# The first two token groups' activation on ScalarE and GpSimd, in place of one VectorE operation, with a new order of issue

## The chip, the cores and the metric

One core of one Trainium2 chip runs the kernel. The metric is the device time of one execution in microseconds (us); lower is better. Five engines work in parallel, each through its own queue in program order: PE (TensorE, matmuls; its weight loads are listed as PEld), DVE (VectorE), ACT (ScalarE), POOL (GpSimd) and SP (SyncE, which here issues the DMAs). They meet through semaphores.

## What is computed

A gated linear attention with complex decays, followed by a two-layer block with a leaky activation. Shortened:

```python
# q, k, v, a_re, a_im: (B, H, S, D) = (4, 8, 768, 48)
mag = np.sqrt(a_re * a_re + a_im * a_im)
scale = np.minimum(mag, 0.999) / (mag + 1e-06)
a_re_n, a_im_n = a_re * scale, a_im * scale
for t in range(S):
    new_re = ar * S_re - ai * S_im          # ar, ai: row t of a_re_n, a_im_n
    new_im = ar * S_im + ai * S_re
    S_re, S_im = new_re + outer(k[t], v[t]), new_im
    y[t] = q[t] @ S_re
x = y.transpose(0, 2, 1, 3).reshape(3072, 384)   # tokens x (heads * D)
h = x @ w_in                                      # w_in: (384, 2048)
g = np.maximum(h, 0.0) + alpha * np.minimum(h, 0.0)
return g @ w_out                                  # w_out: (2048, 384)
```

## The kernel before

**Tasks.** The program is a set of Python generators. Each `yield` marks a step: the engine, a size for a planner and what the step waits for. The code after it issues the step's instructions. The planner itself is not in the file, only its result: ORDER, a string of some 4,500 letters, one letter for each step. `Plan.run` walks the string and advances the task of that letter, so the string fixes the order in which every engine's queue gets its instructions. The yielded sizes and the `Ring` objects (buffer counts) do nothing at run time. Waits on the chip come from the tiles that the instructions read and write.

The letters: A to I are the nine gate tasks (decays and phases of a batch's tokens); J loads q, k, phases and decays of each unit; K and L load rows of v; M brings in the pieces of the weights and alpha; N and O turn the weights' 64-bit words into float32; P to m are the 24 attention units of 128 tokens each; n loads x; o is the two-layer block (`all_mlp`); p and q belong to the last three groups, which are computed by another scheme with fewer multiplications.

**Units.** A unit multiplies q and k by phases and decays on VectorE (tiles KQ, WQ; L742, L744, L797), forms masked products of q and k level by level on TensorE (ps_lv, L759), masks them (A; L773, L782), transposes k (ps_kt, L868), updates the state (ps_kv, L880; St, L916 on ScalarE and L918 on VectorE) and gathers the unit's output in ps_y (L900, L930). The output is copied (L944) and sent to DRAM (ysc), from where a group's x is loaded (xT).

**The two-layer block.** Tokens are handled in groups: `sizes = [1, 1, 2, 2, ...]` units of 128 tokens, so groups 0 and 1 have 128 tokens and the others 256. For a group m and each of 16 slices f of the 2048 features, `features` issues three matmuls into ps_h (L978, two buffers), a ScalarE relu of -h into the group's place in g_sb (L985), and one VectorE operation (L987) that multiplies this by the column `al_1` (1 - alpha) and adds h from PSUM: relu(-h) * (1 - alpha) + h is the activation. Then `outputs` issues the matmul of the slice before (L997, into ps_o) that adds its part to the result. In `all_mlp` the output matmul of f-1 stands behind the ps_h matmuls of f. From group 1 on, the first output matmuls belong to the group before.

**GpSimd's work.** Before the change it has a step of the weights' conversion (L596), small products of the gate tasks (L396, L416, L418, L477, L480, L488, L490, L492; of these, the larger forms run on VectorE), memsets, and sums in the last three groups (L1160).

Of the kernel before, what the change touches and what calls it, by code (L numbers as in the profile page):

```python
# [27 lines left out]


ORDER = (  # L30
    "AAJMMAABAJAAAAAAAAAAAAAAAAAAAAMMMBJMAAAAAAAAAAKANAOAAAABAAANAAAKANNNABAMAJNBKOAKBOOKAABMAKABAAALOAAB"
# [3 lines left out]
    "OCNOOLCNOPCNKOMNNCPQPDJCQDLCDNQPPDQQQLCDQDKQQMCLNDQDOKPQQMODQLOOJQJDKQJDOLCQnOJOLDDJQNJOQLQLOOoLoDDC"
    "QLoQRQoLQQLQooooQQCoQDKNJooooRoMQoQCRCCoooooQoRDQQQCODDCONNCooRQRLoDCLRoMoLoCRRLCoooooCJoRDKCRKooooo"
    "RCDoRQLCDLCoooCoRKoOLCDJCQDCCoLDCRRDDCooooooLCQCooCLCoCoCoLCLCCCLCRCCLCKOCRCRLoCooCRRRCRRoRRCoCRCQQC"
    "CRCQCCoRKCRQRQQCQOORRoRCCQCCooRRCNQDoLoDLoNoDNoooNDoEDNNoEOJoDJRJDRLoooooDDoLDRRRLDRRLRDNDNEJDJSDDRo"
    "oJDESDEDSRDRJESSnJSoLESDoLoLODJSSJDSDLLTSDJoELoooooSSSDLoLooooJSSoDDDoSEDLoooSToSoJooJSSSDoSSDSSoooo"
    "ooSTSDETooooTToSEEoEDoooooSDToSEDTSESSSSDooLDTLoooLEEDSLToLSLoooooDLELoTJDSSSDoooooTTSDSESSSLoDooooo"  # L40
    "SEEDTLLoTKoooooDDDToTEJLDDDDoooooTEUJTDKoDoooKTToDoLoToooTLoUoDJoTLToooToEJoDonooToDEoDTKoUoDJooToUo"
    "EoEUTUEoETEDDDJTooUooDoUUoDooToToTTDoLoLoULoLDULLoooUUoDoLooooDoULoLoELooooLoUULoTLUTLJoooooFUEUoETT"
    "TUUUUTTTUooooTToUETUUFEoUEooooEoUVoUEoooooVVKJJUUEUUEUUoFooLEFLoUoLEUFJVUELoVJoUJooooVJEoFVEJEVoEUoo"
    "oUUUEVoEUoLoVVLEoooEoLEoVEJooooJVEWoFEnVVLoVELoLoooEoKVVEoELVEoJFooooJWoVoVFooWLooLVVEEWoLWVoLWVEFJV"
    "VVJEooVoVoooEKoWKoJEoooVEWWooVWoVoEFWVVVEVVEWELWEELooFEELoWLEoEoLoWWLVLoWEEEEVLLooooooLWEWLEoLEFELEK"
    "FFVVVooWooLooVVVVVFFFVLXKEoEWooooooEWWEEWWJoWWJoooWoEJWoWJoFJWoEWFFWWWWoEoELoLEoJoLoEoFXEooooFooooXo"
    "ooooKXWXLXFWoXoGGXLoXooooJWoLXoLWoFWXoXWFXWoFWXFWWoWXoXFFoFLoXoGFJFnGooooXXoJFoFLoLXXXXLGFLoooooXLFX"
    "XXoGoLFGFLoooooooFXoooGFoJoYJXoJFoJXFGKoooXFYFXoXFYJFooooGXXXYoYXLYFooLXFYFKoLoYoYLXXFZLFXLoXYXFLoXX"
    "XoooYXoFGLGFYYLoYGoFJoYFYJoooFoFZoLFoJoYJGKooooFJGYFYLooYYYLoJYYZGLLFoooooZLoFGYZYZoYZYKJFZZooooYFoZ"
    "YoYFGZYYFYFFYYFZFLFZFFLoYLoooZLooLoFFFFFYFZLFZYYYLFoZLYYFLYoooFZYLaZFLoFoooZZZZoYZZLZoGYFFLLoooZoZGo"  # L50
    "LGoFZJoZFFFGJoooooFooZFFZZFZZZGLoonoFLooLaoFoLoooaJoLoZoaJGoLZooaJaGoaoHoLZZLaaZoHGGoGZGZGGaZLGaLooo"
    "ooaZGaLoaJoZaZaooooGJoHaooHGoooaoaGLaHoooLoGLaaJaHoaJaaJoooooHoGbaoaGHoooaoGaobbJKHoaGaoaoaGaaHoLKoG"
    "JoboLGobLGoLGoooGbLoHGHbLboJbHoGJLaoLbbGLooooGoGHobLGaLaHbLGbabLaabaaGoLaooooLGbboGoGHbGooooJbGbGGKo"
    "bbboJobJbGGbcbbJobGGoooboGcbooooGbGoHbGbGcbbbLGcGLoooGbLcGHcGGJoboJcoLJGGGobLGccLGoobKcbLobHLbobbLoc"
    "obHoGHGdbLGHooooccocGoJoJHoooLcocdJooLconJHLoooocLcHoccccoccLGoJdcGGooocodHocHoHdHoHcGGGcoooGooocGGc"
    "GccccodGLLoooGcodooooLoddJoooLocdoLoIHIoHLdooooLHooLHdcoLdcoLdcLocJHcocddoHoHooKcoooILdocoLHoIHdcdLH"
    "LddoIKdooooJdoIddJoddKdHoHooodoHdoIoHedHHodeHIdddodoHLeHLoLoIHodLHoHLHeIHoLdLoooeeJHeHLoLdddHoooeeoH"
    "JHdedHLoJooooeIoLIeLeoeJddoLHoooLeeoLoHdIHeodJoHIHoooeeoJeeeeoeJeoeIJeoenJHIHoooeJIoeooHeHoHfeeoeHfe"
    "eoLLHoHHJHoHHeHoLfeoLILJHHHHofLooooofeLHfeHfLeHKoeIeLoKffLeHoooooefHeoeLgIIfogJLooooIoooffofoHJILooo"
    "ooHLffoJIoJfHHoooooKHofofJooLfffffofKoJgooHofgIoooggoIHIofofHIoIIoofoHKfooHofogfffoffggoLHLoLogoLoHI"  # L60
    "oLgoooILofnoIfgLgLgLfffoLggJoLgfKoooofooooIgLogfooLfIfofggggggogoohgogIhhLJJJIIhIooooogogoIIoogggggg"
    "oLILogoJIoJgIohJgIILgIgooohLIIgoJgIoIghILhIoIghILoLhhIooooIoIhIoJoLihILJooohhohLoLohLohoooLioJIIoLho"
    "LoJiJooohohooJhhiohhihJhihnoIIIhIoIIhIIIIooohIoIhIioIhihhhhhIihoLihLLLohhhLIIIIIiooooLohhiILiIoLiILo"
    "hLoooiiIoLohihohoLIoooILiIiLoLiiiiiioJioJioIIiIoooioiojoioIiiijIiiJooLojLoJoIoJoLjoooiLoIioLojIjiiiI"
    "jiiooooojjooooLojLiiJoooojLopoLjojiiLoooJjoLoojjJLojLLoooooJojLojooJjjjjjJojjJopjojookkkoojojooojjkj"
    "jojjokLkoLkLokJokoLokLoLoookLjooLjkJkokLLokkLoooLokooooLojjjLokjkjojkjjkojkkLlkookkopkJokJpoookokook"
    "oklkkkkLkLoookJlooLoLolooJokJopoJoLllJklnkLllokoooooklolokooollkkLLLolkoololoooJoLloJoLoooLlmlololoo"
    "oloLoLlooolLmooomololloolpmooolomlomopoomoomomoooomooomoollllllmmomoolomomoooolmoonoolllmmomlmomlmol"
    "lomomoooooooomLooLooooLoLoooLoooooooLoqLoooLooLomLooooLooLooLomLoooooooopooooomoooomoooooooooooooooo"
    "oooooooomomomoomoomomoooomomomoqlmqlmqmmmqqmqoooooqqoqoooooqoqqoqooqoqqooqoqqoqoqooqooqqoooooqoqqoqo"  # L70
    "ooooooooooqoooqoooqqoqqoqooooooooooqqooqoooooqqoqqoqooqoqooqoqqoqqqqqqqqoooooooooooqoqqoqoqooqooqooq"
    "oqoqooqoqoqoooqqqoqqonoooooooooooooooqooqqoqoqqoqqooooooooooooqqoqoqoooqooooooooooooqqqooqooqoooqoqq"
    "oqooooooooqqoooooooooqoooooooooooqooqoooqqoooqoqqqoqooooooooqoqoooqoqooooqqoqqoqooqoqooqqqoqoqqqqqqq"
    "ooooqoooooooqoqqoqooqqqoqoqooooooooooooqqqqqqoqqoooooooooooooooooqqqqoqqoqqooooooooooooooooooqoqqqoq"
# [30 lines left out]
def kernel(  # L105
# [863 lines left out]

    def features(m, f):  # L970

        n = sizes[m] * P
        for kk in range(NK):
            e = yield PE(n * 1.68e-3, ("x", m), ("w_in", f), takes=() if kk else (R["h"],))
            if kk == 0:
                p = ps.tile([P, MT], F32, tag="h", name="ps_h", bufs=2)[:, 0:n]
# [1 line left out]
            nc.tensor.matmul(p, lhsT=w_in_sb[:, f // 2, kk, f % 2 * P:(f % 2 + 1) * P], rhs=x_of[m][:, kk],  # L978
                             start=(kk == 0), stop=(kk == NK - 1))
# [5 lines left out]
        nc.scalar.activation(gt, p, AF.Relu, scale=-1.0)  # L985
# [1 line left out]
        nc.vector.scalar_tensor_tensor(out=gt, in0=gt, scalar=al_1[:, f:f + 1], in1=p,  # L987
                                       op0=ALU.mult, op1=ALU.add)
# [272 lines left out]
```

## Time and profile before

| | |
|---|---|
| time, median of 3 runs | 823.86 us (821.32 to 829.38) |
| profiled execution: time | 820.38 us |
| profiled execution: span from first to last instruction | 818.6 us |
| TensorE matmul busy | 681.1 us (83%), 11680 instructions |
| TensorE weight load busy | 539.0 us (66%) |
| VectorE busy | 693.9 us (85%), 1191 instructions |
| ScalarE busy | 520.3 us (64%), 1307 instructions |
| GpSimd busy | 222.2 us (27%), 293 instructions |
| mean granted TensorE clock | 0.968 |
| shares of the chain of waits that ended last | PE 65%, DVE 14%, DMA 10%, ACT 4% |

How to read what follows: a row of the profile names the line of the kernel, the engine, the operation, the tile written and the tiles read with their shapes, the count, then busy us and mean ns of one, then the engine's idle time just before such operations and what ended it. A duration can overlap the next one of the same engine, since operations are pipelined; the distance between two starts is what one occupies. The forty digits of a slice view are tenths of busy time in forty equal parts of the span. A chain of waits is followed back from the last instruction: each piece is what the next one had to wait for.

### The profile page before, as it was taken

What the parts mean: (1) busy time and instruction counts of PE and PEld (TensorE: products, weight loads), DVE (VectorE), ACT (ScalarE), POOL (GpSimd) and SP (SyncE); (2) the same over time, 40 slices, a digit from 0 to 9 for tenths busy, and PEclk for the clock granted to TensorE, in tenths of its full rate; (3) what the DMA queues carried; (4) which work ended last, traced back from release to release, by engine and by line L of the source; (5) the groups of instructions that cost most, each with busy time, mean ns of one, the idle gap of its engine ahead of it and who ended that gap; (6) DMA issues with size and microseconds to landing.
All of it is one profiled execution on the core that took longest, in us unless ns stands there. A gap on an engine that the chain in (4) does not pass through costs nothing.

```text
span 818.6 us, 27870 instructions
## 1 busy us (share of the span) xinstructions
PE 681.1 (83%) x11680; PEld 539.0 (66%) x11680; DVE 693.9 (85%) x1191; ACT 520.3 (64%) x1307; POOL 222.2 (27%) x293
## 2 busy tenths in 40 slices
PE   0003128659998999999999999999999999999997
PEld 0003126537776777767777777777777777899997
DVE  5999999999989899999999989998787775456574
ACT  8777998669666777876876697555756544312121
POOL 7231343051604310531245054003200000233342
PEclk9999659979999999999999999999999999999999
DMA  8594895593689589738865867787566622101000
GB/s 242 176 294 128 266 296 158 177 253 101 182 235 197 140 194 272 174 90 279 195 168 141 253 160 180 223 197 184 117 182 134 153 77 56 44 1 40 1 21 20
DMA packets 186598, 130.99 MB, mean 160 GB/s; under 512 B 74728, under 2 KB 176872, under 8 KB 186088
## 3 DMA queue, kind: packets, MB, share of 16 engines
q1 hardware_dynamic: 186472, 129.20, 59.3%
q8 instruction: 92, 1.51, 0.8%
q14 instruction: 34, 0.28, 0.1%
HBM read 100.82 MB, written 35.71 MB: 167 GB/s over the span
## 4 chain that ended last, share of the span: by engine, by line
PE 65%; DVE 14%; DMA 10%; ACT 4%; SPq 2%; issue 2%; POOL 1%; DVEq 0%; ACTq 0%; POOLq 0%
PE ps_o L997 19%; PE ps_h L978 18%; PE ps_m L1172 7%; PE ps_lv L759 5%; PE ps_y L1097 4%; PE ps_h L1097 4%; PE ps_y L900 3%; DVE KQ L797 2%; PE ps_kv L880 2%; PE ps_y L930 2%; DMA VL<-in_v_dram 2%; DVE gate L507 2%; PE ps_kt L868 1%; DVE gate L416 1%; DMA T<-decs 1%
## 5 line engine op out<-in xcount | busy, mean ns | idle before, releaser
L978 PE MATMUL ps_h<-xT,w_in_sb 128*128 128x256 f32 (+1 forms) x960 | 227.0, 369 | 2.1 <-DVE w_in_sb L600 1.6
L997 PE MATMUL ps_o<-w_out_sb,g_sb 128*128 128x384 f32 x576 | 222.1, 501 | 4.8 <-DVE g_sb L987 4.7
L978 PEld LDWEIGHTS ps_h<-xT,w_in_sb 128*128 128x128 f32 x960 | 170.9, 195 | 51.3 <-DVE w_in_sb L600 2.2
L797 DVE TENSOR_TENSOR KQ<-KQ,T 96x1024 f32<-96x1024 f32 x120 | 148.4, 1237 | 25.8 <-PE ps_lv L759 19.2
L997 PEld LDWEIGHTS ps_o<-w_out_sb,g_sb 128*128 128x128 f32 x576 | 102.5, 191 | 44.9 <-DVE g_sb L987 6.5
L985 ACT ACTIVATE g_sb<-ps_h 128x256 f32<-128x256 f32 (+1 forms) x160 | 57.9, 362 | 73.0 <-PE ps_h L978 72.2
L759 PE MATMUL ps_lv<-WQ 96*32 96x32 f32 x2304 | 34.4, 203 | 83.6 <-DVE WQ L742 70.2
L759 PEld LDWEIGHTS ps_lv<-WQ 96*32 96x32 f32 x2304 | 26.3, 116 | 105.9 <-DVE WQ L742 71.0
L916 ACT ACTIVATE St<-St,T 96x48 f32<-96x48 f32 x352 | 84.0, 325 | 4.6 <-DVE St L918 4.3
L987 DVE SCALAR_TENSOR_TENSOR g_sb<-g_sb,al,ps_h 128x256 f32<-128x256 f32 (+1 forms) x160 | 71.3, 446 | 13.7 <-ACT g_sb L985 13.1
L1160 POOL TENSOR_TENSOR sums<-g_sb 128x128 f32<-128x128 f32 x48 | 21.8, 475 | 185.5 <-DMA VL<-in_v_dram 110.6
L416 POOL TENSOR_TENSOR gate<-gate 128x72 f32<-128x72 f32 x42 | 34.5, 822 | 133.7 <-ACT gate L446 130.9
L596 POOL TENSOR_SCALAR top<-top 128x768 f32<-128x768 f32 x16 | 44.1, 2755 | 74.6 <-ACT top L588 63.2
L820 ACT COPY WQ<-KQ 96x1024 f32<-96x1024 f32 x48 | 50.0, 1041 | 18.9 <-DVE KQ L797 18.3
L416 DVE TENSOR_TENSOR gate<-gate 128x576 f32<-128x576 f32 (+5 forms) x84 | 50.7, 604 | 1.1
L900 PE MATMUL ps_y<-A,VL 64*48 64x64 f32 x2304 | 41.9, 220 | 4.4 <-issue 4.3
L900 PEld LDWEIGHTS ps_y<-A,VL 64*48 64x48 f32 x2304 | 39.0, 122 | 6.8 <-issue 6.7
L507 DVE TENSOR_TENSOR gate<-gate 128x1152 f32<-128x1152 f32 (+2 forms) x36 | 42.8, 1220 | 0.8 <-POOL gate L492 0.7
L1135 ACT ACTIVATE rl<-g_sb 128x256 f32<-128x256 f32 x24 | 10.0, 416 | 50.0 <-DVE g_sb L1128 50.0
L773 ACT ACTIVATE A<-ps_lv,columns 128x64 f32<-128x64 f32 x144 | 37.4, 336 | 6.2 <-PE ps_lv L759 5.9
L836 ACT COPY W<-KQ 96x512 f32<-96x512 f32 x48 | 30.8, 641 | 16.2 <-DVE KQ L797 8.7
L759 PE MATMUL ps_lv<-KQ,W 96*32 96x32 f32 x1536 | 24.7, 204 | 18.5 <-ACT W L836 17.4
(168 smaller groups left out, 1355.7 us busy)
## 6 DMA issues: line engine op xcount, KB each, us to landing
T<-decs SPq DMA_DIRECT2D x48, 384.0 KB
PP<-phs SPq DMA_DIRECT2D x24, 387.0 KB
KQ<-in_q_dram SPq DMA_DIRECT2D x48, 192.0 KB
decs<-gate SPq DMA_DIRECT2D x7, 1152.0 KB
phs<-gate SPq DMA_DIRECT2D x14, 576.0 KB
KQ<-in_k_dram SPq DMA_DIRECT2D x40, 192.0 KB
vsc<-in_v_dram SPq DMA_DIRECT2D x48, 144.0 KB
VL<-vsc SPq DMA_DIRECT2D x48, 144.0 KB
```

What stands on the lines that cost most here:

```text
L416: on(4 * k).tensor_tensor(out=m, in0=w[:, 1::-1].unsqueeze(2).to_broadcast([P, 2, 2, k]), in1=pairs_of(u), op=ALU.mult)
L507: TT(out=m[:, a], in0=U5[:, 1 + a], in1=turned(off3, o)[:, a].unsqueeze(1).unsqueeze(3).to_broadcast([P, L // 2, nb, 2]), op=ALU.mult)
L759: nc.tensor.matmul(t[64 * i + j:64 * i + j + HC // 2, p], lhsT=keys(n, g), rhs=queries(n, g), start=True, stop=True)
L797: nc.vector.tensor_tensor(out=x, in0=x if x0 is None else x0, in1=m, op=ALU.mult)
L900: nc.tensor.matmul(o, lhsT=Vp[h][64 * i:64 * i + 64, s, e_ * D:(e_ + 1) * D], rhs=a, start=False, stop=False)
L916: nc.scalar.activation(St[:, n], before[:, n], AF.Copy, scale=T[0:D2, n, TL - 4 + s:TL - 3 + s])
L978: nc.tensor.matmul(p, lhsT=w_in_sb[:, f // 2, kk, f % 2 * P:(f % 2 + 1) * P], rhs=x_of[m][:, kk], start=(kk == 0), stop=(kk == NK - 1))
L985: nc.scalar.activation(gt, p, AF.Relu, scale=-1.0)
L987: nc.vector.scalar_tensor_tensor(out=gt, in0=gt, scalar=al_1[:, f:f + 1], in1=p, op0=ALU.mult, op1=ALU.add)
L997: nc.tensor.matmul(sums[0], lhsT=gt[:, c * P:(c + 1) * P], rhs=w_out_sb[:, f], start=(f == 0), stop=(f == NF - 1))
L1097: nc.tensor.matmul(o, lhsT=lhs, rhs=rhs, start=(at in (0, 5)), stop=(at in (4, 8)))
L1172: nc.tensor.matmul(banks[k][:, half], lhsT=lhs, rhs=rhs, start=(j == 0 and half == 0), stop=(j == NF // 2 - 1 and at in (2, 3, 5, 6)))
```

## The change

For groups 0 and 1 (`m < ASIDE`) VectorE's operation is left out. Beside the relu, ScalarE copies h from PSUM into one of two halves of a new SBUF tile, `beside`, after which the ps_h buffer is free. GpSimd multiplies the relu's result by the column, in place, and then adds the copy. That is one ScalarE and two GpSimd instructions more and one VectorE instruction less for each of 2 x 16 slices. The small tile that a first, otherwise unused ScalarE activation wrote is now a part of `beside`. The string ORDER is another one throughout: 4607 letters in place of 4543, the 64 added ones being steps of task o.

```diff
+ASIDE = 2
...
 ORDER = (
-    "AAJMMAABAJAAAAAAAAAAAAAAAAAAAAMMMBJMAAAAAAAAAAKANAOAAAABAAANAAAKANNNABAMAJNBKOAKBOOKAABMAKABAAALOAAB"
...
+    "AABBMJAAAAAAAAAMAAAJAAAAAAABAAAAAAAAAMMMAAAAAABABAAKAANJAABKAKOAAAANMAAKBAAJNNAAKOAAKNOOMANBAABKABAN"
...
-        lv=2, misc=1, y=1, h=2, o=1).items()}
+        lv=2, misc=1, y=1, h=2, o=1, hc=2).items()}
...
-    nc.scalar.activation(consts.tile([P, 1], F32, tag="first", name="first"), bias_two, AF.Abs_reciprocal_sqrt)
+    beside = consts.tile([P, 2, P], F32, tag="beside")
+    nc.scalar.activation(beside[:, 0, 0:1], bias_two, AF.Abs_reciprocal_sqrt)
...
         nc.scalar.activation(gt, p, AF.Relu, scale=-1.0)
+        if m < ASIDE:
+            ra, r = r, (yield ACT(n, takes=(R["hc"],)))
+            hc = beside[:, f % 2, 0:n]
+            nc.scalar.copy(hc, p)
+            R["h"].put(r)
+            yield POOL(1.4 * n, ra)
+            nc.gpsimd.tensor_scalar(out=gt, in0=gt, scalar1=al_1[:, f:f + 1], scalar2=None, op0=ALU.mult)
+            r = yield POOL(1.4 * n, r)
+            nc.gpsimd.tensor_tensor(out=gt, in0=gt, in1=hc, op=ALU.add)
+            R["hc"].put(r)
+            return gt, r
         r = yield DVE(n + 45, r, first=True)
         nc.vector.scalar_tensor_tensor(out=gt, in0=gt, scalar=al_1[:, f:f + 1], in1=p,
                                        op0=ALU.mult, op1=ALU.add)
```

More of the change, by code (lines that the diff above doesn't have):

```diff
@@ L35 @@
[L35 to L74, printed above, removed]
@@ L75 @@
-    "oqoooooooooooooooooqqooooooooooooqoooqoqoooqoqqoqqoooooooooooqqqooooooqoqqoqqooqoqooqoqqqqqooooooooo"
-    "ooqoqqoqooqoqooqqoqqqqqqqqqqqqqqqqqqqqqqqqq")
+    "AABBMJAAAAAAAAAMAAAJAAAAAAABAAAAAAAAAMMMAAAAAABABAAKAANJAABKAKOAAAANMAAKBAAJNNAAKOAAKNOOMANBAABKABAN"
+    "KANOKAOMLALABBNNLBAAOLAAAKABBLOAAKBBLAABAAMAABLAAAKBALAABBBLAAAAABAOOABAAMBANAAAAAKALBAAABABABBBNBNB"
+    "OCNCBJBNNOLJBOKBONBOOBNBNOCBOBCPCPPJKKMKKBCLBBMBCPKBPKCLBBBPPBBBPOLBBJBPCLJOBPBPCOOKBPBBJBPPBCCPBPCB"
+    "PPBBBNPCBCPPNNBPMMKBBBCPPJPBBBBPBPCPPBPBPBCPPBCBBBBBPCBPPBPPCCLCBBBLLBPBNLPCLNLONCNPPPDONNJDCOCLCNOJ"
@@ new lines @@
+    "COOJMCCNCNJCNOCJOCQDKCLCDMQDCJPDNNQDMNQQCDQNJDQPOQQDOQPPPOOPCJDQQLNQKDCKODQJNnLNNMDDCOLQLQRJOLQoOLLD"
+    "DQKQOOoMQKoQQQKoRQooQCQKooQooQoCQDKQooCoooQCDoooCRDDooCROooQoooRoRDCCCODRoooooooQoQoCRRoooCooCRoQoLC"
+    "RRDJooRQCLooCDLCoCoLCoRoCJooCLQooooooLCRQLCCCLCCCDLooCRCoooooCLCDCOLCDRLoCoCOJoLoooooRRooCCCCDLCDoRR"
+    "RCooooooRCRRQQRRQCCDCCooCQoCCRLCQRoRCQooooOORQQCCJCRCRRRRooCRoQNRDNDNDNDNNDRRLDEoEDLDRJOJDoRJDRoJoDO"
+    "oooRLDoooooDnNELLoDSJDENJRooDESDooooooDSRDRJESSJoLSLSoJSSJDLooooSDJJTSSDLESKoSDLEKSooSoJoooooESJDooT"
@@ new lines @@
+    "DJDLDDDoooSoSSSSSSEooooDKSSSDKoTooLEELTKSLEoooooTTTLoTooEDEoooooSoSTEEDEoooooooSooSDTSoSSSDLTooSLoDo"
+    "oLTDoToDoSLTooLoooLDDoSSLoSoDLooSDSEoSoSSoSooLDEoLDDDoooooTDoLooUJTooooLoToJEJUTJTELTLDDDooTJoooooTT"
+    "TDLoTnoooooooooDDoEEEUoooEDTToooDoUoTDDooooUUoUToDTEDoEooooooTooEEoTDDDToUTJoDoooooooooTToLoDDDLoUoo"
+    "LDoUDoooooLoooooUTULoUTooLULooLUoULEoUFoooooULToUTEJUUTLTLUooToEFToTTUoEUTELoULUEoooooUoEUVooooUoEUE"
+    "FJVVoFJEJoooooUoEUJUEUJoUUEoLFUKoEoJVEoLoEVLEJoooUUVLEFVEUVKUoULVoELoUUVVEUooooELoEVEoKooooVEWoJFEVV"
@@ new lines @@
+    "LoEJooEoWEnoLoVLoELooooLoVVLFVJJEoEoooooVoWVFLELoooVVWoJVoJWoEWEVEVooVEVWVoVoooEWWoVFoVEWoooooVEEVEV"
+    "EVEEVFFFWEEWVLWoLWLEEEoKWWELoooooVELoWLoELVEooooKEoELoWFFJVWLVWEVLoEFKoooLWVoEVoWEEEWoWLVVVEWLoWWLWo"
+    "oooVoFLoEoFJJoooWoWoFoWEFFWWoWEWWLLEJFJooooooXJoEoooJXoFooooXKoLWXLoooooWXJFXGXLLWWWoLXXoGXWWooooooX"
+    "FXoFXWooFWWXFWoLoXXFoFFoLXoJGooonoFoJYXGLXoFLoJXXGoooooXFXoXLGoLXXFGLooooXFoXLFooGoooFXYoJXoJFoJoYGF"
+    "oooooooFoJXoFoXFXXFXXYXoLGXLYYLoYLoFoLFGoFLLXXXFYYoLXFXFoooXFXXYFoXoZoYFYoYGYJFLooooJFYYoFLFZoFLoGLo"
@@ new lines @@
+    "ooFYoLFGoLoGYKoYLYYYYKGJZJFYFYKFooooooZZFKoZGJYYYJFoooJFZYoYoFoFFZZYFZYYFYFYYFZFZYLoFZGLLFFFYZLLZZLo"
+    "oooooLYYYFFFFoFZLFYFLYYoooLZaoFZLFLZFZLYGoooooZFZYZYZZLooooZGoLZoFZFFoFnZJGJaJFooooooZoZZFFZZZGLFLGo"
+    "ooooFooaFLooooooaLZaoaJGZJoooaLoJoGoaaHHGoLaGLLooaZZZaLGaZGLoZZJZoGGaooGaaoLGHLaLZGZoooooooHaaKGoooG"
+    "aaHoaoooaoaGaoLHaaaGJHoooooboaoHGoooaoGbbJJKoHoaoGaHaaaaGLooLoGJoboJGobGJGoLGHHLbLooooobHabJoGbLGoLo"
+    "ooLGbboGLoGHbGoLaLHbaGLbabLaabGaLoaaooooGbbLoGoGHbGJoGJooobGbcoJoKbbbbbbooGboobGoGHboooboGbGcJobKoob"
@@ new lines @@
+    "GcbbbboGLbcLGoHbLccLoGcoJoJGbboGLbGccJGbooLboGcGoGbbboboHcLcGGGoccGJccJoooooodLGLcLnJHHoHooooooGcHHL"
+    "cGcLGoccJooococdGoLoKdoLcGGGGHdJHcoooooodHLoGdHKccoooHGHoooGcocooGoGcooGcccccGoLoodGLooooJddoLcodoLc"
+    "LHIoLdooooooIHdLHodLcccoJHoLcdcocLcoLHocddodoILLHcoooooIoHdLdoHILdJdJdooooJHdoddJoHddIodooodHodoHIoH"
+    "doHIedddddooeLLoHeJoHoLIodHJHHKoHeoooHeKIdHeLeLHoodddoooHLeeHLHdedHoLdLIeLILooooooeeHeLHodLooooJHeeo"
+    "doHdeLoHLoooHeeoeeeeoeeJoeHeHJfoeJIHJHoooeoHJeHHoHIHoIeofIeeeoeeHoHLILoJoHeoJHHHfeoLnILHHHfLeeeoHLoo"
@@ new lines @@
+    "ooeIeoKHfefLoefeHIeoHLffHooooLoHogHJoLfLoooofJgoooofofIJfKHLooooffoHoHfLoIHKLooooooLonIIoooJgoJoHogK"
+    "gffgffoffffooofIfoHfoogfHofIoooIfggIIgIfHffffgfHoLoJoLofLoooHLooLofHgogLfgLfLooILoLggfofogoofoooffJL"
+    "ILgIogooggggfoggLogLIoIIoogogohooohhJJJJIoogogogIgIggggogLhoJgoLgohJoggLoggIghoILoogIhLIhJLIhILIoJIo"
+    "oooooLIhhILIohIJLooooohIioLIhoJhooLIhIoJoJioIJohhKoIoooIKIioLIoJohioIIoooIhLohiLhhioohhhohihhohIoIIi"
+    "oohohoIiIIojohoIIihhhhhIooLIIILhoIIIiILohoILoILiiILoIoLhhhIoLiIoLoLiioLohIiLhoLIhhLooooohihiLoiiiiio"
@@ new lines @@
+    "IioooipJioJioJoiojiooooiiiiiioLoIIIIijoLooojILiooLoLjjoLIIoiiioJjioLjLoIjLJoooooiijLJooooojoIjiiojoo"
+    "IjoLoLojjLoLojLiooooooJjojooJjjjjjojJjonoJojJjJkoooojojkoojojkjjjjokoLjLkjkLokLooJkkoJoLkLooooLkojoL"
+    "koLkjkLjLkkoookojooojoLlkokLjoojjkokjkkLokkLlokkokJoookJopkJoJookookkkkkkoLkLolLooLolLoLoookLolJlkJl"
+    "kLollLoJolkkooooolplklookklkoooooololooomoooloooooooooJlolLooJpoLoLooLloLlLllnoooollomoolloolmooomom"
+    "omolmolommooomlopmlllllomLmoLmLolLooLmmolLmooooooolmomolmlolmlolmoloomooooomomnooLoooooLoLpLLoLooolo"
@@ new lines @@
+    "LomooooooooomLopoqoooomoooooooooooooomomoooooooooooooooooooooooooooooooomomomoomommomoooooomomoqmqmq"
+    "mmmqqmqloooooqqoqooqoooqoqqqoooopooooqqoooooooqoooqoqqooooooooooqooqooqqooooqoqqoqooqoqooooooqqooooo"
+    "qoooqonqqoqooqoqqooqoqoqqqqqqoooooooooooqoqqoqooqoqooqqoqooqoqqqqqoqooqqooooooooqooqoqooooooooooooqq"
+    "qoqqoooooooooooooooqooqqqoqqoqqqoooooooooooqooqqooqoqoooqqoqqoqooqoqooqqqoqooooooqooqoooqoqqoooooooo"
+    "oooqqoooqooooqoqqooooooooooooooqooooqoqqqoqooqoqooqoqoqqqqoooooooooooqoqqoqooqqoooooqqooqooooooooqoq"
@@ L79 @@
+    "qoqqqoooqoooooooooooooqqqqqqoqqoooooooooooooooooqqqqoqooooooooooooooooqqqooooqoqqoqoooooooqqooqqoooo"
+    "ooooqoooooooooooooooooooqqoqoqoqooqqooqoqqqqqqqoooooooooooqoqqoqooqoqooqqoqqqqqqqqqqqqqqqqqqqqqqqqqq"
+    "qqqqqqq")
 class Ring:
```

3 lines of the change are left out of this document (removed).

## The prediction

> **What bounds the kernel now.** I read the slices first, then the busy time by stage, then the chain of waits, then the rows of the operations involved, and last the moments at which GpSimd and VectorE meet.
>
> ```profile
> PE   0003128659998999999999999999999999999997
> ...
> DVE  5999999999989899999999989998787775456574
> ACT  8777998669666777876876697555756544312121
> POOL 7231343051604310531245054003200000233342
> ```
>
> A slice is 20.5 us. VectorE is full from the second slice, TensorE from the eleventh (about 205 us). By stage (columns: busy us and instructions of PE, PEld, DVE, ACT, POOL, then clock, DMA share, GB/s):
>
> ```profile
> 120.00:205.00 85.00, 64.27 (x1337) 50.30 (x1327) 83.26 (x150) 65.78 (x166) 26.16 (x23) 0.90 0.63 171
> 205.00:245.00 40.00, 39.16 (x729) 30.97 (x728) 36.79 (x53) 26.18 (x81) 13.11 (x10) 1.00 0.71 209
> 245.00:682.00 437.00, 429.91 (x7974) 321.28 (x7974) 391.39 (x564) 297.69 (x801) 98.92 (x121) 1.00 0.68 174
> 682.00:819.00 137.00, 132.23 (x1076) 123.44 (x1072) 74.82 (x209) 32.74 (x106) 42.98 (x96) 0.99 0.09 27
> ```
>
> The changed operations run from 122.7 us to about 243 us: the first group (m=0) in the first row, where VectorE idles 1.7 of 85 us and TensorE 20.7, the second (m=1) in the second row, where TensorE idles 0.8 of 40 us. After 245 us TensorE idles 7.1 + 4.8 us in all. So time is won only by letting TensorE reach its full stretch earlier, and lost by anything that stops it after 205 us.
>
> The chain of waits between 118 and 262 us (start, length, what) says the same, in pieces:
>
> ```profile
> 142.69 0.26 DVE g_sb L987
> 142.94 0.09 DVE run L418
> 143.06 0.18 DVE gate L416
> 143.24 0.26 DVE g_sb L987
> ...
> 195.63 1.80 ACT St L916 x8
> 197.43 0.93 ACT WQ L820
> ```
>
> Up to 190 us it is VectorE's queue, from 190.7 to 202.6 us ScalarE's, then DMA issues on SyncE, and from 216 us TensorE. The removed operation, L987, is a link of it in 13 pieces up to 190 us: nine of 0.26 and four of 0.35, 0.33, 0.34 and 0.06, with the first at 123.39 us; 3.4 us together.
>
> The rows to cost with (line, engine, operation, count, busy us, mean ns of one, idle before):
>
> ```profile
> L480 POOL TENSOR_TENSOR gate<-gate 128x126 f32<-128x126 f32 x12 | 11.0, 915 | 0.9
> ...
> L987 DVE SCALAR_TENSOR_TENSOR g_sb<-g_sb,al,ps_h 128x128 f32<-128x128 f32 x32 | 10.7, 335 | 0.1
> ...
> L490 POOL TENSOR_SCALAR gate<-gate 128x144 f32<-128x144 f32 x6 | 9.0, 1506 | 0.5
> ...
> L985 ACT ACTIVATE g_sb<-ps_h 128x128 f32<-128x128 f32 x32 | 8.8, 276 | 2.2 <-PE ps_h L978 2.1
> ```
>
> **The change, part by part.** *Removed: 32 VectorE operations.* Their row says 335 ns, but the next one starts 0.26 us after each (143.24, then 143.50 on the chain), so VectorE gets 32 x 0.26 = 8.3 us back, 3.4 us of it on the chain. Take -3.4; bounds -8.3 and 0 (if the DMA and ScalarE pieces after 190 us end last anyway).
>
> *Added: 32 copies on ScalarE*, of the relu's size and source (276 ns; the relu occupies 0.16 us on the chain, as at 192.57 and 199.43 us). In all 32 x 0.28 = 9 us beside 92 us of ScalarE work in 120 to 245 us. On the chain only the ScalarE stretch counts: four relus lie in it, so four copies, 4 x 0.16 = +0.7. Bounds 0 and 4 x 0.28 = 1.1; if ScalarE became the limit throughout, 9.
>
> *Added: 64 operations on GpSimd*, a multiply by a column and an addition for each f. Neither shape is in the trace before. For the multiply the nearest row is L490 (144 elements), which took 0.31 us at its shortest and 1.51 on average; for the addition L480 (126 elements), 0.42 and 0.92, with the four additions of the last groups (L1160) at 0.46 where VectorE is less busy. A pair costs 0.77 us at least and 2.4 us at most. Why the spread, two moments show (GpSimd, then VectorE):
>
> ```profile
> 211.77 2.10 POOL L490 TENSOR_SCALAR gate<-gate 128x144 f32<-128x144 f32 x1
> ...
> 284.16 0.31 POOL L490 TENSOR_SCALAR gate<-gate 128x144 f32<-128x144 f32 x1
> ```
>
> ```profile
> 211.51 1.25 DVE L744 TENSOR_TENSOR KQ<-KQ,PP 96x1024 f32<-96x1024 f32 x1
> ```
>
> ```profile
> 283.81 0.48 DVE L987 SCALAR_TENSOR_TENSOR g_sb<-g_sb,al,ps_h 128x256 f32<-128x256 f32 x1 [0.61 <-ACT g_sb L985]
> ```
>
> Begun beside L744, which reads two SBUF tensors, the multiply took 2.10 us; begun beside L987, whose second input is in PSUM, it took 0.31. GpSimd waits for VectorE's two-SBUF-input operations, and the 32 operations that go are some of the few during which it did not have to.
>
> VectorE pays too. Against the median of its own form, VectorE's operations beside the twelve L480 were longer by 2.0 us in all, 0.17 us for each; beside the sixteen 128x768 multiplies (L596) by 9.1 us, 0.57 each, scaled to 128 elements 0.09; beside the six L490 nothing. A pair therefore takes 0.17 to 0.26 us from VectorE; I take 0.22, as L480 is the closest in kind and size. For the 13 pairs on the chain that is +2.9 (bounds 0.5, from the smallest additions, L416 and L418, at 0.014 and 0.021 us each; and 3.4), so VectorE gives back nearly what it was relieved of.
>
> The Trainium skill ("SBUF — State Buffer", section Who interferes with whom) speaks against this change: a VectorE instruction with two SBUF inputs and a GpSimd one that reads SBUF exclude each other wholly, whichever starts first, while a VectorE instruction with at most one SBUF input does not collide. The trace agrees on GpSimd's side (2.10 against 0.31 us); on VectorE's side it shows 0.17 us for an addition of 0.42, not all of it.
>
> *New waits.* GpSimd works in order, and so does TensorE. The output matmul of f (L997) now follows relu, copy, multiply and addition, but stands behind the three ps_h matmuls of f+1, so it has one round of f as slack: 85/16 = 5.3 us in the first group, 40/16 = 2.5 us in the second. Behind it on TensorE waits all attention work. The copy of f+2 waits for the addition of f (two halves of the new tile); behind it queue ScalarE's gate, state and relu work. GpSimd's own work of 26.2 us in the first stretch leaves ample room (16 pairs at 2.4 are 38, together 65 of 85). In the second, 13.1 us leave 26.9 us for 16 pairs: 1.68 us a pair is the most that goes unseen. Halfway between 0.77 and 2.4 is 1.6, just below. I take +1.0 for single late pairs; bounds 0 and 14 (16 x 2.4 + 13.1 + 2 for gaps, against 40). The ps_h buffers come free after the copy instead of after VectorE's turn; TensorE in 118 to 160 us waited 4.8 us for L987, where it is not the limit, so I count nothing; without that cover it would be at most those 4.8 won.
>
> *The order.* Up to the first matmul of group 2 the old string has 1119 letters, the new 1186: 64 are new o steps, and of the rest TensorE has 199 and 201 steps, the SyncE tasks J, K, L, M and n together 178 or 179, VectorE 374 and 344 (32 removed, two more), GpSimd 48 and 112. At the first matmul of group 0 it is 494 and 495 letters. Unit 0's last matmul step comes 34 letters later, but its transposed result only 5 (454 and 459) and the load of x one (476 and 477), so nothing that group 0 needs moves. Later units lie within some six matmul steps. It is the same plan with small swaps. A swap's price no row gives: TensorE's 7.1 us of gaps from 245 to 682 us is the most that a better order can win there, and I let a worse one lose as much; value 0.
>
> *Sum* against the profiled execution (span 818.6, time 820.38): -3.4 + 2.9 + 0.7 + 1.0 + 0 = +1.2, or 821.6. The profiled execution lay 3.5 us below the median of the three runs, 823.86; on that scale 825.
>
> **Rivals.**
> *1, the relief is real (faster).* If GpSimd slips in beside ps_kv, ps_lv and ps_h readers at 0.77 a pair and VectorE pays only 0.035 a pair, the chain loses 3.4 and up to 8.3 us: 820.5 to 815.6, and below with a luckier order. For it: VectorE idles 1.7 of 85 us, and the measured toll beside short GpSimd operations is nearly nothing. Against: the chain is not VectorE's after 190 us.
> *2, TensorE waits for GpSimd in the second group (slower).* At the mean rows, 2.4 us a pair, GpSimd needs 53 us where TensorE needs 40: +14, 838. It decides from 1.68 us a pair. For it: L490's mean, and VectorE is 92% busy there. Against: the smallest times are a quarter of that, and the first group has room.
> *3, VectorE is shut out for whole GpSimd operations.* Then each pair takes 0.77 us from it: 13 x 0.77 - 3.4 + 0.7 = +7.3, 831. The Trainium skill's rule, named above, would have it so when GpSimd starts first. Against: 0.17 us measured beside L480; for: 0.31 beside the 128x288 L492 and 0.57 beside L596.
>
> **How the numbers follow.** Chances: forecast 0.45, relief 0.25, TensorE waiting 0.20, VectorE shut out 0.10. The 80% range reaches from 813 (relief in full, 815.6, with some of the order's gain) to 838 (rival 2). About 1%, 8 us, is what can be told from no change: faster means below 815.6, slower above 832.1. Half of rival 1 (0.12) and the forecast with the order's gain and the relief of 4.8 us (0.08) are faster: 0.20. Rival 2, half of rival 3 (0.05) and the forecast with the order's loss (0.05) are slower: 0.30. The rest, 0.50, is no change.
>
> **What would show it.** In the changed profile: VectorE's busy time in 120 to 245 us down by some 5 us or less; VectorE's L797 and L742 beside GpSimd above 1.22 us; the new GpSimd rows between 0.4 and 1.3 us each, more than their shortest; waits of ps_o on GpSimd of 1 us in the second group if I am right, 10 if rival 2 is. TensorE's full stretch should begin within 2 us of 205. I am wrong in the mechanism if the additions take about 0.46 us throughout, or if TensorE's gaps after 245 us move by more than the whole sum: then the order decides, not the moved work.

## The result, and the profile after

The changed kernel takes 850.68 us (median of 4 runs, 849.49 to 856.91) against 825.35 us for the kernel before: a ratio of 1.0332, 95% interval 1.0284 to 1.038. It is 3.3% slower and lies outside the stated range, whose upper end was 838. The profiled execution took 849.65 us; its span is 847.7 us.

The relus of the first groups show where the time went. The table has the start in us of the first relu of a group, from ScalarE's timeline:

| | group 0 | group 1 | group 2 | span |
|---|---|---|---|---|
| before | 122.7 | 185.4 | 221.8 | 818.6 |
| after | 126.0 | 192.6 | 249.5 | 847.7 |
| later by | 3.3 | 7.2 | 27.7 | 29.1 |

Of the 29.1 us, 24.4 are lost while the two changed groups run, 20.5 of them in the second. The slices of the changed kernel (21.2 us each):

```profile
PE   0004038746789999998999999999999999999997
...
DVE  5999998996759989998998999898795676555573
...
POOL 6231355768850430152143123204200000323342
```

GpSimd is the engine that fills up (slices 6 to 12), and VectorE and TensorE empty beside it. By stage, with columns as in the prediction; the work after 245 us is divided where the last three groups begin:

```profile
120.00:205.00 85.00, 56.73 (x1072) 43.11 (x1072) 72.29 (x103) 58.90 (x155) 57.99 (x59) 0.76 0.66 177
205.00:245.00 40.00, 31.76 (x652) 25.25 (x644) 30.21 (x42) 22.91 (x73) 33.51 (x36) 0.91 0.30 71
245.00:711.00 466.00, 453.43 (x8376) 340.13 (x8380) 405.94 (x583) 314.52 (x855) 96.25 (x125) 1.00 0.68 176
711.00:848.00 137.00, 132.32 (x1076) 123.52 (x1074) 77.12 (x217) 32.66 (x104) 42.76 (x96) 1.00 0.08 25
```

From 120 to 245 us GpSimd is busy 91.5 us, before 39.3. VectorE, which was to be relieved of 8.3 us, falls from 120.1 to 102.5 us, by more than that, because it has to wait itself; TensorE falls from 103.4 to 88.5. The two new GpSimd rows and the longest waits between 120 and 250 us (engine, tile, line, what it waited for: us in total, times, longest):

```profile
L995 POOL TENSOR_SCALAR g_sb<-g_sb,al 128x128 f32<-128x128 f32 x32 | 36.9, 1152 | 17.6 <-ACT g_sb L988 13.5 <-ACT runs L447 1.7 <-DMA gate<-in_a_im_dram 1.6
...
L997 POOL TENSOR_TENSOR g_sb<-g_sb,beside 128x128 f32<-128x128 f32 x32 | 23.3, 729 | 6.4 <-ACT beside L992 4.3
```

```profile
PE ps_o L1011 <- POOL g_sb L997: 19.5, 13, 5.3
DVE KQ L800 <- PE ps_lv L762: 16.7, 5, 7.4
...
PE ps_h L981 <- ACT beside L992: 6.6, 1, 6.6
```

Before, the same matmuls waited for VectorE's operation, in the same window:

```profile
PE ps_o L997 <- DVE g_sb L987: 4.7, 7, 1.8
```

A pair (one multiplication and one addition) takes 1.15 + 0.73 = 1.88 us on average. TensorE's output matmuls wait 19.5 us for the addition, 13.8 of them in the second group, and VectorE then waits 16.7 us for what TensorE does later: a stall of the two-layer block has become one of the attention units, since all share TensorE's queue. The chain of waits in the second group (start, length, what) runs through GpSimd:

```profile
206.74 0.29 ACT g_sb L988
207.03 0.09 issue
207.12 2.81 POOL g_sb L995
209.93 1.57 issue
211.54 1.08 POOL g_sb L997
212.66 0.91 PE ps_o L1011 x2
```

### The profile page after: what moved, and what is told of

Read it like the earlier page. It is cut to its first block, busy times and chain, and to the rows that moved or that the text cites. A ratio compares the mean times of both kernels' runs of the same rounds, so it can differ in the third digit from the quotient of the medians.

```text
span 847.7 us, 27955 instructions
## 1 busy us (share of the span) xinstructions
PE 688.5 (81%) x11680; PEld 544.0 (64%) x11680; DVE 692.6 (82%) x1159; ACT 525.5 (62%) x1339; POOL 274.9 (32%) x357
## 4 chain that ended last, share of the span: by engine, by line
PE 65%; DVE 9%; DMA 7%; POOL 6%; ACT 6%; issue 4%; SPq 2%; POOLq 0%; DVEq 0%; ACTq 0%
PE ps_o L1011 20%; PE ps_h L981 18%; PE ps_m L1186 6%; PE ps_lv L762 4%; PE ps_h L1111 3%; PE ps_y L1111 3%; PE ps_y L903 3%; PE ps_kv L883 2%; PE ps_y L933 2%; DVE KQ L800 2%; PE ps_kt L871 2%; DMA T<-decs 2%; POOL top L599 1%; DVE gate L510 1%; POOL g_sb L995 1%
## 5 line engine op out<-in xcount | busy, mean ns | idle before, releaser
L1011 PE MATMUL ps_o<-w_out_sb,g_sb 128*128 128x384 f32 x576 | 227.5, 510 | 20.1 <-POOL g_sb L997 19.5
L981 PEld LDWEIGHTS ps_h<-xT,w_in_sb 128*128 128x128 f32 x960 | 175.4, 198 | 68.6 <-DMA xT<-ysc 7.8
L419 POOL TENSOR_TENSOR gate<-gate 128x72 f32<-128x72 f32 x42 | 38.8, 924 | 132.3 <-ACT gate L449 129.8
L1001 DVE SCALAR_TENSOR_TENSOR g_sb<-g_sb,al,ps_h 128x256 f32<-128x256 f32 x128 | 60.6, 473 | 25.8 <-ACT g_sb L988 25.7
L995 POOL TENSOR_SCALAR g_sb<-g_sb,al 128x128 f32<-128x128 f32 x32 | 36.9, 1152 | 17.6 <-ACT g_sb L988 13.5
```

What stands on the lines that cost most here:

```text
L419: on(4 * k).tensor_tensor(out=m, in0=w[:, 1::-1].unsqueeze(2).to_broadcast([P, 2, 2, k]), in1=pairs_of(u), op=ALU.mult)
L1011: nc.tensor.matmul(sums[0], lhsT=gt[:, c * P:(c + 1) * P], rhs=w_out_sb[:, f], start=(f == 0), stop=(f == NF - 1))
```

## The experiments

Each is compared with runs of the kernel before on the same chip; the ratio's 95% interval stands in brackets. Two theories were set against each other: **W**, the work moved to GpSimd costs the time, and **O**, the new order does.

**The new order with the old operation.** In groups 0 and 1:

```diff
-            ra, r = r, (yield ACT(n, takes=(R["hc"],)))
...
-            R["hc"].put(r)
+            yield ACT(n)
+            yield POOL(1.4 * n)
+            r = yield DVE(n + 45, r)
+            nc.vector.scalar_tensor_tensor(out=gt, in0=gt, scalar=al_1[:, f:f + 1], in1=p, op0=ALU.mult, op1=ALU.add)
             return gt, r
```

> The new order with the old operation: VectorE's multiply-and-add is issued at the step where the change issues GpSimd's addition; no copy, no GpSimd work. If the moved work costs the 27 us (theory W), this runs at 820 to 830 us and TensorE's first relu of group 2 is back near 222 us. If the new order itself is slow on the chip (theory O), it stays at 843 us or more. In between, 830 to 843, both have a part.

Measured: 836.97 us against 823.09, 1.018 (1.0117 to 1.0244). Both theories have a part. The group starts are 125.3, 188.8 and 232.1 us: group 2 is still 10 us late.

**The old order with the new operation.** The copy behind the relu, both GpSimd instructions at the step of the old VectorE operation (the tile `beside` is made as in the change; `...` stands for that):

```diff
...
+        if m < 2:
+            hc = beside[:, f % 2, 0:n]
+            nc.scalar.copy(hc, p)
+            r = yield POOL(2.8 * n, r)
+            nc.gpsimd.tensor_scalar(out=gt, in0=gt, scalar1=al_1[:, f:f + 1], scalar2=None, op0=ALU.mult)
+            nc.gpsimd.tensor_tensor(out=gt, in0=gt, in1=hc, op=ALU.add)
+            return gt, r
```

> The old order with the new operation: copy right behind the relu, multiply and addition on GpSimd at the step of the old VectorE operation. Theory W: 840 to 860 us, with waits of ps_o on GpSimd of 10 us or more. Theory O: 820 to 830 us.

Measured: 850.11 us against 823.09, 1.0341 (1.0294 to 1.0389), as W expects. TensorE's wait for the addition between 100 and 250 us:

```profile
PE ps_o L1005 <- POOL g_sb L992: 22.0, 12, 8.1
```

The first relus of groups 1 and 2 start at 199.75 and 251.0 us, 14.3 and 29.2 us later than before, so in the old order half of the loss falls in the first group. So the moved work alone, with no change of order, costs as much as the whole change; the new order saves nothing that can be told.

**The copy directly behind the relu.** In the changed kernel up to six other ScalarE steps stand between them.

```diff
-            ra, r = r, (yield ACT(n, takes=(R["hc"],)))
             hc = beside[:, f % 2, 0:n]
             nc.scalar.copy(hc, p)
+            ra, r = r, (yield ACT(n, takes=(R["hc"],)))
```

> The changed kernel with the copy issued directly behind the relu instead of up to several ScalarE instructions later. In the changed kernel TensorE waited 7.2 us for one late copy, at 181 us. If late copies are a part of the cost of their own (theory C), this gains 5 to 8 us, 843 to 846 us. If GpSimd's queue sets the pace anyway (theory W), it gains less than 3 us, 848 or more.

Measured: 849.92 us, 1.0325 (1.0275 to 1.0376). TensorE's wait of 6.6 us for the late copy is gone, a wait of 6.6 us for a piece of the weights stands in its place, and the time is the same. Late copies (theory C) are no cost of their own here.

**Without the multiplication.**

```diff
-            nc.gpsimd.tensor_scalar(out=gt, in0=gt, scalar1=al_1[:, f:f + 1], scalar2=None, op0=ALU.mult)
```

> The changed kernel without GpSimd's multiply in groups 0 and 1 (the factor 1 - alpha is left out there), so GpSimd has one operation a slice in place of two. Theory W, by GpSimd's time: half or more of the 25 us comes back, 830 to 840 us, since the multiplies are 36.9 of the 60.2 us of the pairs and the longest of them (4.3 and 3.5 us) stand on the chain. If it is not GpSimd's time but its place in the order that counts (its additions queued behind gate products and conversions), less than 6 us comes back, 845 or more.

Measured: 839.96 us, 1.0213 (1.0165 to 1.0262). Removing half the instructions returns 10 of the 27 us, at the weak end of what W expects.

**The old operation earlier in the new order**, at the step behind the relu, since the order alone had put it where GpSimd's addition was (the edit is against the run of the order alone):

```diff
-            yield ACT(n)
-            yield POOL(1.4 * n)
-            r = yield DVE(n + 45, r)
+            r = yield ACT(n)
             nc.vector.scalar_tensor_tensor(out=gt, in0=gt, scalar=al_1[:, f:f + 1], in1=p, op0=ALU.mult, op1=ALU.add)
+            yield POOL(1.4 * n)
+            yield POOL(1.4 * n)
```

> As the run of the order alone (new order, old operation), but the VectorE operation is issued at the step right behind the relu, two steps earlier than there. The order alone took 837 us with 12.3 us of waits of ps_o on VectorE between 100 and 250 us. If the lateness of that step was the cost (theory L: the steps were spread for GpSimd), this runs at 824 to 831 us. If the rest of the order is worse on the chip (theory O), it stays at 834 or more.

Measured: 835.77 us against 823.9, 1.0144 (1.0073 to 1.0216). Theory L falls: the order costs some 12 to 14 us with the operation at either of the two steps.

**GpSimd in group 0 only**, group 1 with VectorE's operation:

```diff
+            if m == 1:
+                yield ACT(n)
+                yield POOL(1.4 * n)
+                r = yield DVE(n + 45, r)
+                nc.vector.scalar_tensor_tensor(out=gt, in0=gt, scalar=al_1[:, f:f + 1], in1=p, op0=ALU.mult, op1=ALU.add)
+                return gt, r
```

> The changed kernel with GpSimd's operations in group 0 only; group 1 uses VectorE's operation, issued at the step of GpSimd's addition. Between the first relu and that of group 2 the changed kernel loses 24.4 us, about 4 of them in group 0 and 20 in group 1. If GpSimd's load in group 1 is the cause (theory W, second group), 12 to 16 us come back, 835 to 839 us. If the damage is done in group 0 and only shows later, 845 or more.

Measured: 842.51 us, 1.0237 (1.0165 to 1.0309). Group 1's pairs are worth about 8 us, less than the 12 to 16 expected. Neither alternative fits: group 0's share is not small.

**The small products of gate tasks D and E on VectorE**:

```diff
-        tiny, tiny_engine = (DVE, nc.vector) if g < 3 else (POOL, nc.gpsimd)
+        tiny, tiny_engine = (DVE, nc.vector) if g < 5 else (POOL, nc.gpsimd)
```

> The changed kernel with the small products of gate tasks D and E on VectorE in place of GpSimd, so GpSimd's queue holds the pairs and little else. If the pairs wait mostly behind gate products in GpSimd's queue (theory Q), 6 us or more come back, 845 us or less, although VectorE gets 60 operations of 0.1 to 0.4 us more. If the pairs are slow by themselves (theory P: blocked by VectorE), it is 848 us or more.

Measured: 844.88 us, 1.0267 (1.0188 to 1.0346). About 5 us come back with 48 operations moved. The intervals of this run and of the change overlap, so the size is uncertain; the place behind gate products (theory Q) is a part of it, and TensorE's wait for the addition falls from 19.5 to 14.6 us. The timelines of ScalarE and GpSimd in the changed kernel show how, for the first slice of group 1:

```profile
192.59 0.26 ACT L988 ACTIVATE g_sb<-ps_h 128x128 f32<-128x128 f32 x1
192.75 0.26 ACT L992 COPY beside<-ps_h 128x128 f32<-128x128 f32 x1
```

```profile
191.73 1.33 POOL L419 TENSOR_TENSOR gate<-gate 128x72 f32<-128x72 f32 x1
193.14 2.27 POOL L421 TENSOR_TENSOR gate<-gate 128x36 f32<-128x36 f32 x1
...
199.73 0.26 POOL L421 TENSOR_TENSOR gate<-gate 128x36 f32<-128x36 f32 x1
199.97 0.60 POOL L995 TENSOR_SCALAR g_sb<-g_sb,al 128x128 f32<-128x128 f32 x1
```

Relu and copy are done at 193.0 us, but six gate products stand in front of the multiplication, which starts at 199.97 us. With these products on VectorE the multiplication of this slice starts 0.36 us after its relu (192.20 against 191.84 us).

**GpSimd only writes.** The arithmetic of the two operations is left out; the copies on ScalarE stay:

```diff
-            nc.gpsimd.tensor_scalar(out=gt, in0=gt, scalar1=al_1[:, f:f + 1], scalar2=None, op0=ALU.mult)
+            nc.gpsimd.memset(gt, 0.5)
             r = yield POOL(1.4 * n, r)
-            nc.gpsimd.tensor_tensor(out=gt, in0=gt, in1=hc, op=ALU.add)
+            nc.gpsimd.memset(gt, 0.25)
```

> The changed kernel in which GpSimd only writes a constant twice per slice (the multiplication and the addition are left out in groups 0 and 1), so that its two operations read nothing, take about 0.2 us each and do not wait for the copy. The place in the queues and the rest stay. Theory P (the pairs are slow because they read beside VectorE's two-input operations): 832 to 840 us, what the order alone costs. Theory Q (the place behind other GpSimd work): 845 or more.

Measured: 835.8 us against 823.9, 1.0154 (1.0071 to 1.0236), the cost of the order alone. GpSimd's rows and TensorE's waits of this run:

```profile
L997 POOL MEMSET g_sb<- 128x128 f32 x32 | 6.5, 204 | 1.7
...
L995 POOL MEMSET g_sb<- 128x128 f32 x32 | 6.5, 203 | 46.9 <-ACT g_sb L988 44.1 <-DMA gate<-in_a_im_dram 2.7
```

```profile
PE ps_h L981 <- ACT beside L992: 7.4, 2, 7.1
...
PE ps_h L981 <- DMA xT<-ysc: 6.1, 1, 6.1
...
PE ps_o L1011 <- POOL g_sb L997: 3.4, 2, 2.1
```

The shortest, median and longest ns of the second of the two:

```profile
L997 POOL MEMSET g_sb<- x32: 194/204/207, 126.8 to 229.3; 128x128 f32 x32
```

With 0.4 us a pair in place of 1.88, in the same places, ps_o waits 3.4 us in place of 19.5. So the pairs' 15 us in this order are the price of their reading and computing and of waiting for the copy, not of merely passing through GpSimd. None of the 64 writes took more than 207 ns, though by the timelines 37 of them lay for their whole length beside VectorE operations with two SBUF inputs, the kind that held up the reading ones. The 32 copies on ScalarE cost nothing here that can be told from the order's cost. What remains is the order's: TensorE waits 6.1 us for x of group 0, and 7.1 us for one copy.

**One slice more of lead** for the output matmuls of both groups:

```diff
+        held = []
...
-                made[m, f] = new
+                held.append(((m, f), new))
+                while len(held) > (1 if m < ASIDE and (m, f) != (ASIDE - 1, NF - 1) else 0):
+                    key, value = held.pop(0)
+                    made[key] = value
```

> The changed kernel in which, in groups 0 and 1, the output matmul of a slice stands one slice further back on TensorE, so that each pair on GpSimd has two rounds in place of one. If TensorE loses time because a pair now and then is late by some us (theory J, single delays), 6 us or more come back, 845 or less. If GpSimd cannot keep up over the stretch (theory P, its total time), a longer lead changes little: 847 or more.

Measured: 847.48 us against 824.14, 1.0275 (1.0235 to 1.0314). TensorE's waits from 100 to 250 us:

```profile
PE ps_lv L762 <- ACT W L839: 17.6, 7, 5.6
...
PE ps_h L981 <- DVE w_in_sb L603: 10.0, 2, 7.6
...
PE ps_o L1011 <- POOL g_sb L997: 5.2, 3, 3.0
```

The wait for GpSimd falls from 19.5 to 5.2 us, the time by 3 to 5 only: waits for attention copies (17.6 us, in the changed kernel 10.5) and weights (10.0 us, there 1.1) have grown instead. Single delays (theory J) are a small part. The time is the one that theory P expects, but P's reason does not fit: between the first relus of groups 1 and 2 GpSimd is busy 45.4 of 56.9 us in the changed kernel, so it is not full.

**Old start, new rest**, and **old until group 2, new after**, and the reverse, **new until group 2, old after**; all with the old operation. The edit in each is the string ORDER: its first part from one order, then the other order without the steps already done.

> Old operation, issued right behind the relu; old order up to the first matmul of group 0, from there the new order with what is left. The new order with that operation took 836 us, the old 824. In the new order x of group 0 came some 3 us later (relu at 125 to 128 us, before 122.7). If the late start of group 0 is the order's cost (theory S), this runs at 826 to 830 us. If the rest of the order is (theory R), at 832 or more.

> Old operation; old order up to the first matmul of group 2, from there the new order. Shows what the new order's later part costs. The runs with the new order had 4 to 5 us more TensorE gaps between 250 and 680 us than the kernel before. If these belong to the later order (theory R2), this is 827 to 831 us; if they are consequences of the disturbed start, 822 to 826.

> Old operation, issued right behind the relu; the new order up to the first matmul of group 2, from there the old one. The old order up to there and the new behind it took 828.6 us, 4 more than the kernel before. If the parts of the order add up (theory A), this takes 824 + 12 - 4, 830 to 834 us. If the new order's first part costs all of the 12 by itself, 834 or more.

Measured: 837.52 us, 1.0181 (1.0138 to 1.0223), for the old start; 828.57 us, 1.0049 (1.0023 to 1.0074), for the old order until group 2; 829.83 us against 821.91, 1.0091 (1.0051 to 1.0131), for the new one until group 2. The old start gains nothing, but this does not settle the late start (theory S): in that run TensorE no longer waits for x, yet the first relu of group 0 still comes at 126.15 us (before 122.72), behind weight conversions and gate work in ScalarE's queue. So a late x is not what costs; a late first relu may be. The order's two parts add up, 0.9% + 0.5% beside 1.4 to 1.8% for the whole: some 7 us up to group 2, and 4 us after.

**Two operations in one GpSimd instruction**, first in the multiplication, then also in the weights' conversion, then the latter in the kernel before:

```diff
-            nc.gpsimd.tensor_scalar(out=gt, in0=gt, scalar1=al_1[:, f:f + 1], scalar2=None, op0=ALU.mult)
+            nc.gpsimd.tensor_scalar(out=gt, in0=gt, scalar1=al_1[:, f:f + 1], scalar2=0.0, op0=ALU.mult, op1=ALU.add)
...
-        nc.gpsimd.tensor_scalar(out=top, in0=top, scalar1=F64_SMALL, scalar2=None, op0=ALU.max)
+        nc.gpsimd.tensor_scalar(out=top, in0=top, scalar1=F64_SMALL, scalar2=F64_SMALL, op0=ALU.max, op1=ALU.max)
```

> The changed kernel with GpSimd's multiplication written as multiply, then add 0, in one instruction with two operations. Undisturbed, the multiplication with one operation took 0.60 us, while a tensor-scalar instruction with two operations on 144 elements took 0.31 us in the profile before. If the number of operations makes the difference, the shortest multiplication is 0.3 us, GpSimd gets 32 x 0.3 = 9.6 us back and the time falls by 3 to 8 us, to 843 to 848. If the column operand is what costs 0.3 us, the shortest stays at 0.6 and the time at 850.

> The changed kernel with both one-operation tensor-scalar instructions of GpSimd written with two operations: the pair's multiplication (as in the run before, which took 848.4 us) and the maximum of the weights' conversion, 128x768, which stands in front of the first pairs (4.86 and 4.75 us) and took 2.12 us at its shortest. If the one-operation form is slow for every size, the maximum's shortest falls to about 1 us, and the time by 2 to 6 us, to 842 to 846. If it concerns the multiplication alone, 848.

> The kernel before (old operation, old order) with the same maximum written with two operations, both the same maximum. If the one-operation form is slow, GpSimd needs 10 to 20 us less in the first 165 us and VectorE, which lost 9 us beside these maxima, gets part of that back: 818 to 823 us, a little faster than before. If the form makes no difference, 824.

Measured: 848.41 us, 1.0288 (1.0244 to 1.0332), for the multiplication; 853.59 us, 1.0375 (1.0336 to 1.0414), with both; 823.18 us, 1.002 (0.9993 to 1.0046), in the kernel before. The instructions' shortest, median and longest ns, first the multiplication in the changed kernel and with two operations, then the maximum in the kernel before, as it was and with two operations:

```profile
L995 POOL TENSOR_SCALAR g_sb<-g_sb,al x32: 597/668/4338, 127.2 to 246.5; 128x128 f32<-128x128 f32 x32
```

```profile
L995 POOL TENSOR_SCALAR g_sb<-g_sb,al x32: 370/492/3861, 127.5 to 243.3; 128x128 f32<-128x128 f32 x32
```

```profile
L596 POOL TENSOR_SCALAR top<-top x16: 2125/2351/8044, 14.2 to 162.5; 128x768 f32<-128x768 f32 x16
```

```profile
L596 POOL TENSOR_SCALAR top<-top x16: 2764/3012/8691, 14.4 to 163.0; 128x768 f32<-128x768 f32 x16
```

The multiplication's shortest falls from 597 to 370 ns, the maximum's rises from 2125 to 2764. So the form is not slow for every operation; two maxima cost more than one, and a multiplication alone more than one with an addition. The shorter multiplication frees 11.0 us of GpSimd (274.9 to 263.9 us busy) and brings 2 to 4 us of time, at the weak end of what was expected; the intervals do not tell that from nothing. No run was faster than the kernel before.

## Why the prediction was wrong

Put together, as ratios to the kernel before:

| | old operation | new operation |
|---|---|---|
| old order | 1 | 1.0341 |
| new order | 1.0144 to 1.018 | 1.0332 |

The pairs on GpSimd cost 3.4% in the old order and 1.5 to 1.9% in the new one. The order that makes the pairs cheaper costs the same amount again. The costs do not add up to one list of causes; each cell is a schedule of its own.

**TensorE's wait for GpSimd**, a term of +1.0 us in the sum, is the step that failed most. ps_o waited 19.5 us; in the second group, for which the prediction gave 1 us as its own sign and 10 as that of rival 2, it was 13.8. Rival 2 named the wait, with a chance of 0.20 and a price of 14 us for the second group alone. In the old order the pairs cost 27 us, half of it in the first group; in the new order 12 to 15 us, some 8 of them in the second, so that there the figure of 14 agrees by chance. Three parts of the working led there. First, a pair was put at 1.6 us, just below the 1.68 us from which it decides; it took 1.88. The multiplication's lower bound of 0.31 us came from L490, an instruction with two operations; with one it takes 0.60 at least. The row nearest in size was not the nearest in kind. Second, the stretch up to 205 us was cleared because GpSimd's total there had ample room, and the second group was judged by a total too, 1.68 us a pair. A queue that works in order is late by position, not by total: GpSimd was not full in either group (45.1 of 66.6 us and 45.4 of 56.9, from first relu to first relu), and still ps_o waited 4.0 us before 160 us, and its longest wait, 5.3 us up to 201 us, is for the first slice of group 1, the one behind six gate products. Third, the slack of a round was taken to absorb what came late. With one round more, ps_o's wait shrank to 5.2 us, but the time by 3 to 5 us only.

**The order at 0** was the second failed step, with bounds of 7.1 us each way: it costs 1.4 to 1.8%, 12 to 14 us. The argument was that the letters lie near each other. That unit 0's result and the load of x stand at equal places did not keep the first relu of group 0 from coming some 3 us later, and the rest of the order costs more. Counting steps ahead of a point says what an engine has done by then, not what it waited for. Which swaps cost the 7 us before group 2 is open; TensorE's waits for x (6.1 us) and for a late copy (7.4 us) in the run that only writes are places, and were not tried one by one. The prediction's sign for an order that decides, TensorE's gaps after 245 us moving by more than the sum, was met (11.9 us before, 17.2 after), yet the new operation in the old order lost as much as the whole change: the sign does not tell the two apart.

**VectorE's relief** of 8.3 us was mostly taken back, as forecast, and what was left was worth nothing. Over the whole execution VectorE was busy 693.9 us before and 692.6 after, and 694.6 and 696.2 in the two runs of the old operation in the new order. The net gain is 1.3 to 3.6 us, so the toll of a pair is 0.15 to 0.22 us, an estimate from these four figures; the forecast had 0.22. In the run that only writes, with the same VectorE operations in the same order, it was busy 688.7 us, so 3.9 us of the toll, 0.12 us a pair, come from the reading. Rival 3 (VectorE shut out for 0.77 us a pair) falls by this. But from 120 to 245 us it then idles 22.5 of 125 us, since TensorE holds up its work: the chain's VectorE pieces were replaced by GpSimd's.

**The copies at +0.7**: moving them changed nothing (850 against 850), and the run that only writes still has them and costs what the order alone costs. Both agree with a small price.

**GpSimd blocked by VectorE**, the reason given for the spread, holds, and is stronger than the two moments in the prediction showed. GpSimd's longest multiplication and VectorE's timeline beside it:

```profile
207.12 4.34 POOL L995 TENSOR_SCALAR g_sb<-g_sb,al 128x128 f32<-128x128 f32 x1 [0.34 <-ACT g_sb L988]
```

```profile
207.01 1.35 DVE L292 TENSOR_TENSOR gate<-gate 128x1152 f32<-128x1152 f32 x1
...
208.27 1.35 DVE L366 SCALAR_TENSOR_TENSOR gate<-gate 128x1152 f32<-128x1152 f32 x1
209.54 0.17 DVE L419 TENSOR_TENSOR gate<-run,runs 128x12 f32<-128x12 f32 x1
209.63 1.35 DVE L366 SCALAR_TENSOR_TENSOR gate<-gate 128x1152 f32<-128x1152 f32 x1
210.90 0.16 DVE L421 TENSOR_TENSOR run<-gate 128x6 f32<-128x6 f32 x1
210.98 1.32 DVE L800 TENSOR_TENSOR KQ<-KQ,T 96x1024 f32<-96x1024 f32 x1
```

The multiplication sits through five VectorE operations with two SBUF inputs in a row and ends 0.48 us after the start of a sixth, the last line; why it came through there is open. The other pairs fit: by the two timelines, each of the 22 operations of the pairs that took over 1 us had 0.99 us or more of such VectorE operations beside it, and those with less than 0.25 us of them beside took 0.60 to 0.65 us (multiplication) or 0.45 to 0.46 (addition). The Trainium skill ("SBUF — State Buffer", section Who interferes with whom) has the two exclude each other, the later one waiting until the earlier is done. The trace agrees that GpSimd waits, but not that it waits for one operation: here it did not get its turn between five that followed each other.

## What to carry to other kernels

Before work moves to an engine that has time to spare, follow who waits for its result, and look at what stands in that engine's queue between the pieces of the moved work; the engine's total load says little. GpSimd is a bad link in a chain that TensorE waits for while VectorE runs back-to-back operations on two SBUF tensors: its operations of 0.45 to 0.6 us became 0.7 to 1.2 us on average and 4.3 at worst. When a change brings a new order with it, run the old operation in the new order and the new operation in the old one: the four cells show whether the order pays for the operation.
